# RWKV-6 chunks feeding an MLP on one core: one cumulative-sum matmul instead of two from chunk-batch 8 on, column sums of w_out by one-column matmuls, and a new written-out order

## The chip, the core and the metric

The kernel runs on one core of a Trainium2 chip. The metric is the device time of one execution in microseconds, as the median over five runs. Every figure about a part of the kernel comes from one execution that the hardware profiler recorded.

The core has five engines with a queue each, and every queue runs in order: TensorE (PE; the load of its stationary operand is shown apart as PEld), VectorE (DVE), ScalarE (ACT), GpSimd (POOL) and SyncE (SP), which here issues all the DMAs.

## The reference

```python
# r, k, v, w: (batch 4, heads 8, seq 768, dim 48); u: (8, 48)
state = zeros((B, H, D, D))
for t in range(S):
    cur = einsum('bhd,bhe->bhde', u[None] * k[:, :, t], v[:, :, t])
    y[:, :, t] = einsum('bhd,bhde->bhe', r[:, :, t], state + cur)
    state = w[:, :, t, :, None] * state + einsum('bhd,bhe->bhde', k[:, :, t], v[:, :, t])
x = y.transpose(0, 2, 1, 3).reshape(B * S, H * D)      # 3072 tokens, 384 features
h = maximum(x @ w_in, 0)                               # w_in: 384 x 2048
out = (s * (h * h) + b) @ w_out                        # w_out: 2048 x 384
```

A linear recurrence with a decay w for each channel gives y; an MLP with a squared ReLU follows. `b` is a scalar, so its share of the output is b times the column sums of w_out.

## The kernel before, in words

**Recurrence.** The sequence is cut into chunks of L = 128 steps, six for each of four batch entries: 24 pairs of chunk and entry, called batches n = 0 to 23. Batches 0 and 1 are one double chunk packed together (`packed`); the order of the others goes chunk by chunk over the entries, so batches 20 to 23 are the last chunks (no state is passed on from them: `keep` is false). For each batch:

- `load n.0` to `n.3` (SP, L279 to L308) bring w, r, k and v, 192 KB each (384 KB for the packed pair), in rows of 192 bytes.
- `ln` (ACT, L310): logarithm of w in bf16, `lw`.
- `cum` (PE, L355): cumulative sums of `lw` over the chunk, as two matmuls of 128x384 into one PSUM tile `cums` of two banks: the exclusive sum with `tri_strict` (L383) into bank 0, minus the inclusive sum with `ntri_incl` (L386) into bank 1; and four one-column matmuls (L391) for the chunk's total decay, at the end of bank 0, if `keep`.
- `exp` (ACT, L399): Exp of both, 768 columns, into `E` in bf16 (L404), and Exp of the four columns into `lam` (L408). `l2` (POOL, L431) spreads `lam`.
- `mul` (DVE, L411): r and k times the two halves of `E`, into `prd`.
- `tr` and `tev` (PE L445, ACT L462) transpose `prd`, and from batch 9 on `tev` is a DMA transpose on SP (L477) instead.
- `mt` (PE, L494): the products of k and r of the chunk, into a PSUM tile of two banks; `msk` (DVE, L526) masks them. `cum` and `mt` share one PSUM buffer, tag A, of which there is one: each waits until the one before has been read.
- `ymm` (PE, L537), `yev` (DVE, L621): the batch's y. In `ymm` of the packed pair, the upper 64 rows follow the lower ones.
- `dmm`, `sup`, `st` (PE, DVE, POOL) carry the state; `rkp`, `rku`, `cd`, `yd` (POOL and DVE) make the term with u; `vb` casts v.
- `xtr` and `xev` (PE, ACT) transpose y into the MLP's input `xT`; from batch 12 on `xev` is a DMA transpose on SP (L486).

**MLP.** Two batches make one token tile T (0 to 11) of 256 tokens. `g1 T.i` (PE, L714): six matmuls of 128x256 into `h_ps` (two PSUM buffers); `relu` (ACT, L732); `sq` (L740) squares on DVE or ACT; `g2 T.q` (PE, L758): four matmuls of 128x384 into `o_ps`; `oev` (DVE, L773) and `store` (SP). The weights come as four pieces each, `li` and `lo` (768 KB each), and are cast by `ci` and `co`. The column sums: `colsum` 0 to 3 (L797) multiply an all-ones matrix by w_out, 16 matmuls of 128x384 that leave every column sum in all 128 rows; `csevac` (ACT, L809) scales them by b into `bconst`.

**The order.** The program is not laid out by loops. Each step above is registered with `pl.add` (name, engine, a planned duration, dependencies, and the buffer rings that it takes), from L854 on, and the string `ORDER` (L37) names every step in the sequence in which it is issued. `Plan.order` (L130) walks that string and checks dependencies and rings; each engine gets its instructions in that sequence. `@A`, `@D`, `@P` after a name overrule its engine, and `+8` stands for eight dummy matmuls of 128x256 (`warm`, L1046). Planned durations have no effect on the program once `ORDER` is written. Semaphores between instructions are put in by the tile framework, from the tiles that they read and write.

Names in the texts join step and number: `g10.0` is g1 of tile 0, part 0; `cum22` is cum of batch 22; `A` in "A's next use" is that PSUM buffer.

Of the kernel before, what the change touches and what calls it, by code (L numbers as in the profile page):

```python
# [8 lines left out]
FP32 = mybir.dt.float32  # L9
# [16 lines left out]
PKD = 1.55  # L26
DTK = 9
# [10 lines left out]
load0.0 load0.2 load0.1 load2.0 load_u ln0 ln1 load3.0 +13 cum0 exp0 load3.1 +8 cum1 l20 mul0  # L38
load2.1 load2.2 ln2 rkp0 +2 u_mm load3.2 exp1 tr0 ln3 load0.3 +1 cum2 mul1 tev0 l21 u_ev load3.3
+4 tr1 rkp1 exp2 lo0 tev1 rku1 +4 cum3 exp3 li0 mul2 +9 mt0 rku0 cd1 load2.3 tr2 msk0 rkp3 tev2  # L40
li1 l22 +7 mt1 mul3 vb0@A vb1@A rkp2 msk1 +1 tr3 dmm0 li2 tev3 rku3 sup0 +2 mt2 st0 cd0 co0@A ymm0
cd3 yd0 msk2 load4.0 yd1 ymm1 ci0 yev0 small rku2 xtr0 mt3 yev1 vb2 xev0 +1 xtr1 vb3 xev1 +1 dmm1
l23 li3 +1 dmm2 sup1 g10.0 cd2 ci1 dmm3 g10.1 sup2 relu0.0 msk3 ymm2 relu0.1 lo1 yd2 sq0.0@A g10.2
sup3 sq0.1@A g10.3 yd3 load4.1 yev2 ymm3 load4.2 ci2@D ln4 g20.4 relu0.2 xtr2 yev3 cum4 relu0.3
sq0.2 load5.0 g10.4 xev2 sq0.3@A xtr3 g10.5 ci3 xev3 colsum0 relu0.4 lo2 relu0.5 g20.0 sq0.4 exp4
g10.6 co1 load6.0 sq0.5@A g11.0 relu0.6 lo3 g20.1 relu1.0 g11.1 sq0.6@A mul4 load5.1 g10.7 relu1.1
rkp4 tr4 relu0.7 g11.2 tev4 l24 rku4 load5.2 colsum1 relu1.2 g20.5 st1 cd4 small2 ln5 g11.3
sq1.1@A co2 cum5 sq1.0@A g11.4 relu1.3 sq1.2 load4.3 exp5 g20.2 colsum2 sq0.7@A co3 load7.0 g11.5
ln6 relu1.4 mt4 load5.3 colsum3 msk4 load6.1 rkp5 g11.6 csevac load6.2 relu1.5 g20.6 sq1.3 vb4@A
load7.1 mul5 cum6 g20.7 ln7 sq1.4 load8.0 tr5 exp6 oev0.1 dmm4 g20.3 vb5 load7.2 relu1.6 rku5  # L50
g21.4 oev0.0 tev5 cum7 load6.3 sup4 yd4 g11.7 exp7 g21.0 mul6 load8.1 relu1.7 ymm4 sq1.5@A l26 st2
cd5 mt5 l25 load8.2 rkp6 yev4 tr6 msk5 g21.1 ln8 load7.3 yd5 tev6 g21.5 st3 l27 dmm5 load9.0 rku6
cum8 sq1.7@A sup5 g21.6 exp8 mul7 load9.3 ymm5 vb6@A xtr4 g21.2 st5 st4 yev5 xev4 load8.3 mt6
sq1.6@A xtr5 mul8 tr7 store0.0 xev5 g21.3 tev7 cd6 vb7 g12.0 load10.0 msk6 rkp7 tr8 ln9 dmm6
load12.1 g21.7 rku7 sup6 relu2.0 g12.1 tev8 oev1.1 load11.1 yd6 cum9 cd7 load9.1 relu2.1 g12.2
sq2.0 exp9 l28 ymm6 vb9 load9.2 g12.3 yev6 st6 relu2.2 mt7 oev1.0 sq2.1 store0.1 vb8 g12.4 relu2.3
msk7 yd7 xtr6 dmm7 load11.0 g12.5 xev6 l29 sup7 rkp8 sq2.2@A g22.0 relu2.5 load10.1 dmm8 sq2.3@D
ymm7 ln10 rku8 g22.4 relu2.4 yev7 load12.0 sq2.4@A mt8 sup8 load10.2 st7 g12.6 sq2.5 msk8 g22.5
rkp9 load11.2 relu2.6 xtr7 cd8 g12.7 st8 ln11 load13.0 cum10 xev7 mul9 relu2.7 ymm8 load11.3 g13.0
exp10 rku9 g22.1 relu3.0 load12.2 g13.1 sq2.7 mul10 cum11 ln12 load10.3 dmm9 g13.2 exp11 sq2.6  # L60
tev9 sq3.0 g22.2 relu3.2 cd9 l211 yd8 cum12 relu3.1 sup9 g22.3 ln13 st9 tev10 exp12 g22.6 oev2.0
g13.3 mul11 vb11@A load12.3 g22.7 relu3.3 l212 yev8 rkp10 store1.1 cum13 sq3.1 oev2.1 g13.4 exp13
rkp11 dmm11 tev11 g23.0 sup11 relu3.4 yd9 xtr8 sq3.2@A g13.5 sq3.3 mul12 mt9 load13.1 relu3.5
g13.6 rku11 msk9 xev8 g23.1 load16.0 relu3.6 g23.4 load13.2 st11 vb12@A ymm9 sq3.6@A sq3.5@D mt10
rku10 yev9 sq3.4@A g23.5 msk10 tev12 vb10@A dmm12 l210 xtr9 l213 g23.6 xev9 cd10 g23.2 load17.0
sup12 yd10 g14.0 load14.3 dmm10 mt11 relu4.0 sup10 store1.0 g13.7 msk11 g14.1 relu3.7 rkp13 ymm10
sq3.7 cd11 load14.0 g14.2 st12 relu4.1 yev10 ymm11 relu4.2 mul13 g23.3 load13.3 sq4.1 g14.3 yd11
sq4.0@A load14.1 xtr10 g14.4 relu4.3 rkp12 load14.2 yev11 mt12 oev3.0 relu4.4 g14.5 vb14 tev13
msk12 sq4.4@A rku12 g24.4 relu4.5 xtr11 xev10 g23.7 sq4.3@D load15.0 ln14 cd12 g14.6 xev11
load15.1 sq4.2 vb13@A yd12 oev3.1 cum14 relu4.6 g14.7 load15.2 rku13 sq4.5 ymm12 exp14 dmm13 g24.5  # L70
yev12 cd13 relu4.7 g15.0 xev12 mul14 sq4.6@A g24.0 relu5.0 yd13 sup13 store2.1 g15.1 mt13 st10
load15.3 relu5.1 g15.2 msk13 ln15 l214 g24.6 ln16 store2.0 relu5.2 g15.3 sq4.7@D load18.0 sq5.2@A
rkp15 cum15 ln17 load16.1 g24.1 exp15 st13 dmm14 ymm13 load16.2 relu5.3 rku15 g24.7 yev13 tev14
# [1015 lines left out]
```

## Time and profile before

| | us |
|---|---|
| median of 5 runs | 191.76 |
| the five runs | 191.58, 191.75, 191.76, 191.84, 193.97 |
| the profiled execution, own time | 191.76 |
| its span, first to last instruction | 189.9 |
| PE busy | 182.1 |
| PEld busy | 141.8 |
| ACT busy | 140.9 |
| DVE busy | 124.5 |
| POOL busy | 106.2 |
| DMA: 35.32 MB in 122601 packets, 117329 of them under 512 B | 92.7% of 16 engines' span in queue 1 |

Busy time is a sum of the durations of an engine's instructions, without overlap counted twice. Matmuls are pipelined: each is recorded with its latency, so that the next starts before it ends, and the time for which one holds the engine is read from the start of one to the start of the next. The granted TensorE clock is 1.00 throughout. In lists of groups, a line gives source line, engine, operation, output and inputs by name, shapes and count; then busy time and mean duration in ns; then the idle time of the engine just before, and what ended it. In a timeline a line gives start, duration, engine, line, operation and count, and in brackets an idle time before it.

### The profile page before, as it was taken

Reading aid. Unit: us, or ns where it says so; the run is one execution under the profiler, and the core shown is the slowest. Engines: PE = TensorE matmul, PEld = TensorE weight load, DVE = VectorE, ACT = ScalarE, POOL = GpSimd, SP = SyncE. Lnnn points to the kernel's source line nnn. Section 1 sums busy time; section 2 is a strip of 40 time slices with the busy share of each in tenths; the row PEclk is TensorE's granted clock in tenths of the full one; section 3 lists DMA queues with packets and bytes.
Section 4 is the critical chain, followed back from the end, with each engine's and each line's share of the span. In section 5 each row is a group of like instructions: output and inputs, shape, how many; then the busy total and the mean of one; then the engine's idle time right before and its main releaser. Section 6 shows DMA issues by size and latency. Waiting matters only on the chain.

```text
span 189.9 us, 4916 instructions
## 1 busy us (share of the span) xinstructions
PE 182.1 (96%) x1916; PEld 141.8 (75%) x1916; DVE 124.5 (66%) x198; ACT 140.9 (74%) x268; POOL 106.2 (56%) x138
## 2 busy tenths in 40 slices
PE   6998999999899999999999999999999999999992
PEld 3566898877578786779878777778788777887872
DVE  7348876447669948978686638956577776670242
ACT  3476869988798889958988988749779678483830
POOL 3669773704859965978766696089334677100000
PEclk9999999999999999999999999999999999999999
DMA  6999999989898999999999799899987999630033
GB/s 148 221 202 335 344 327 253 262 221 202 166 179 185 207 169 188 208 174 210 162 209 219 128 207 223 173 196 138 226 165 124 210 164 186 148 109 0 0 128 124
DMA packets 122601, 35.32 MB, mean 186 GB/s; under 512 B 117329, under 2 KB 120530, under 8 KB 122578
## 3 DMA queue, kind: packets, MB, share of 16 engines
q1 hardware_dynamic: 122578, 35.01, 92.7%
q8 instruction: 15, 0.25, 0.6%
q14 instruction: 8, 0.07, 0.1%
HBM read 25.17 MB, written 4.72 MB: 157 GB/s over the span
## 4 chain that ended last, share of the span: by engine, by line
PE 72%; SPq 10%; DMA 6%; DVE 5%; ACT 3%; issue 2%; DVEq 0%
PE o_ps L765 28%; PE h_ps L721 26%; SPq L292 8%; DMA rkt<-in_k_dram 6%; PE mt_ps L516 3%; PE warm_ps L1048 2%; PE y_ps L579 2%; PE trps L450 2%; SPq L841 2%; PE y_ps L570 2%; DVE prd L424 1%; PE cums L368 1%; PE cums L383 1%; PE y_ps L559 1%; PE cums L386 1%
## 5 line engine op out<-in xcount | busy, mean ns | idle before, releaser
L721 PE MATMUL h_ps<-xT,w_in 128*128 128x256 bf16 x576 | 77.7, 273 | 0.0
L765 PE MATMUL o_ps<-w_out,gT 128*128 128x384 bf16 (+1 forms) x400 | 74.7, 320 | 0.1
L734 ACT ACTIVATE rh<-h_ps 128x512 bf16<-128x512 f32 x96 | 56.9, 599 | 23.7 <-PE h_ps L721 22.9
L721 PEld LDWEIGHTS <-w_in 128*128 128x128 bf16 x576 | 60.8, 114 | 7.1
L765 PEld LDWEIGHTS <-gT 128*128 128x128 bf16 x400 | 36.8, 98 | 15.9 <-DVE gT L746 0.2
L744 ACT ACTIVATE gT<-rh 128x512 bf16<-128x512 bf16 x65 | 39.3, 633 | 0.4
L318 POOL TENSOR_TENSOR rkp<-rkt 128x384 f32<-128x384 f32 x22 | 23.2, 1059 | 17.1 <-DMA rkt<-in_k_dram 16.7
L527 DVE TENSOR_TENSOR mt_sb<-mt_ps,tri_strict 128x1024 bf16<-128x1024 f32 x22 | 26.8, 1219 | 7.7 <-PE mt_ps L516 7.7
L424 DVE TENSOR_TENSOR prd<-rkt,E 128x768 bf16<-128x768 f32 x22 | 25.5, 1160 | 9.0 <-DMA rkt<-in_k_dram 6.8
L347 POOL TENSOR_TENSOR yd<-vt,cd 128x384 bf16<-128x384 f32 x22 | 20.7, 943 | 13.3 <-DVE cd L341 7.7
L324 POOL TENSOR_TENSOR rku<-rkp,u_bc 128x384 f32<-128x384 f32 x24 | 27.7, 1162 | 0.4
L404 ACT ACTIVATE E<-cums 128x768 bf16<-128x768 f32 x24 | 19.5, 813 | 4.9 <-PE cums L375 2.4
L624 DVE TENSOR_TENSOR x_sb<-y_ps,yd 128x384 bf16<-128x384 f32 x24 | 13.3, 555 | 13.3 <-PE y_ps L579 9.0
L746 DVE TENSOR_TENSOR gT<-rh 128x512 bf16<-128x512 bf16 x31 | 15.8, 521 | 8.9 <-ACT rh L734 8.9
L776 DVE SCALAR_TENSOR_TENSOR o_sb<-o_ps,s_bc,bconst 128x384 f32<-128x384 f32 (+1 forms) x25 | 14.8, 596 | 8.4 <-PE o_ps L765 8.4
L661 POOL TENSOR_TENSOR st<-stmp,l 128x384 bf16<-128x384 bf16 x16 | 15.6, 978 | 1.7 <-DVE stmp L652 1.6
L437 POOL TENSOR_TENSOR l<-lam,par 128x8 f32<-128x8 f32 x20 | 6.7, 337 | 14.8 <-ACT lam L408 14.8
L313 ACT ACTIVATE logw<-wt 128x384 bf16<-128x384 f32 x22 | 11.4, 525 | 4.3 <-DMA wt<-in_w_dram 4.3
L341 DVE TENSOR_REDUCE cd<-rku 128x8 f32<-128x384 f32 x24 | 13.0, 543 | 2.0 <-POOL rku L324 2.0
L1048 PE MATMUL warm_ps<-warm_sb 128*128 128x256 bf16 x54 | 10.3, 330 | 1.1 <-DVE warm_sb L1005 1.1
L652 DVE TENSOR_TENSOR stmp<-d_ps,st 128x384 bf16<-128x384 f32 x16 | 8.8, 550 | 3.7 <-PE d_ps L611 2.3
L516 PE MATMUL mt_ps<-RK 48*128 48x128 bf16 x176 | 8.7, 219 | 0.0
(90 smaller groups left out, 174.8 us busy)
## 6 DMA issues: line engine op xcount, KB each, us to landing
out_dram<-o_sb SPq DMA_DIRECT2D x23, 192.0 KB, 3.5
wt<-in_w_dram SPq DMA_DIRECT2D x22, 192.0 KB, 4.4
rkt<-in_r_dram SPq DMA_DIRECT2D x22, 192.0 KB, 4.7
rkt<-in_k_dram SPq DMA_DIRECT2D x22, 192.0 KB, 4.6
vt<-in_v_dram SPq DMA_DIRECT2D x22, 192.0 KB, 3.9
wo_st<-in_moe_w_out_dram SPq DMA_DIRECT2D x4, 768.0 KB, 6.5
wi_st<-in_moe_w_in_dram SPq DMA_DIRECT2D x4, 768.0 KB, 8.9
pkt<-in_w_dram SPq DMA_DIRECT2D x1, 384.0 KB, 3.8
```

The lines of the kernel that those rows point to most:

```text
L318: nc.gpsimd.tensor_tensor(out=rkp, in0=c["r"], in1=c["k"], op=ALU.mult)
L324: nc.gpsimd.tensor_tensor(out=rku.rearrange("t h d -> t (h d)"), in0=c["rkp"].rearrange("t h d -> t (h d)"), in1=u_bc, op=ALU.mult,)
L347: nc.gpsimd.tensor_tensor(out=yd, in0=c["v"], in1=c["cd"].unsqueeze(2).to_broadcast([128, H, D]), op=ALU.mult,)
L404: nc.scalar.activation(out=E, in_=ps[:, :, 0:HD], func=AF.Exp)
L424: nc.vector.tensor_tensor(out=prd[:, :, :, 0:D].rearrange("t x h d -> t (x h) d"), in0=c["rk"].rearrange("t x h d -> t (x h) d"), in1=c["E ...
L527: nc.vector.tensor_tensor(out=m.rearrange("s g p t -> s (g p) t"), in0=c["mt_ps"].rearrange("s g p t -> s (g p) t"), in1=(masks[n % 2] if ...
L661: nc.gpsimd.tensor_tensor(out=c["st_new"], in0=c["stmp"].rearrange("q p (g e) -> q p g e", g=2), in1=c["l2"].unsqueeze(3).to_broadcast([12 ...
L721: nc.tensor.matmul(ps[:, f, :], lhsT=w_in_sb[ft // FPP][:, kt, :].rearrange("p (m j) -> p j m", j=FPP)[:, ft % FPP, :], rhs=xT[T][:, kt, : ...
L734: nc.scalar.activation(out=rh, in_=hs[T, i], func=AF.Relu)
L744: nc.scalar.activation(out=g, in_=rh, func=AF.Square)
L746: nc.vector.tensor_tensor(out=g, in0=rh, in1=rh, op=ALU.mult)
L765: nc.tensor.matmul(os_[T, k][:, cols], lhsT=gT[T][:, ft, tt * 128 : (tt + 1) * 128], rhs=w_out_sb[ft // FPP][:, ft % FPP, cols], start=(ft ...
```

## The change

From batch 8 on (`ONE = 8`), `cum` leaves out the second matmul. A VectorE add (`inc`) makes the inclusive sum from the exclusive one in PSUM and from `lw`, and a second Exp (`exn`), with scale -1, reads it from SBUF. The first Exp then covers 384 columns and the four decay columns in one instruction; `E` is fp32 and holds `lam`. The column sums of w_out are made by one-column matmuls, with w_out as the stationary operand, so that the sums lie along the partitions; two small VectorE steps (`cssplit`) split them into two bf16 terms, and six matmuls with the identity (`csspread`) spread them over all rows. `ymm` of the packed pair alternates between the two halves of the rows. The order is written anew.

```diff
+ONE = 8
...
+    cs_sum = const.tile([128, 2, KT], BF16, name="cs_sum", tag="cs_sum")
...
-        nc.tensor.matmul(
-            ps[:, 1, 0:HD], lhsT=ntri_incl, rhs=lw[:, :, 0:D], start=True, stop=True
-        )
+        if n < ONE:
+            nc.tensor.matmul(
+                ps[:, 1, 0:HD], lhsT=ntri_incl, rhs=lw[:, :, 0:D], start=True, stop=True
+            )
...
-        E = work.tile([128, 2, HD], BF16, name="E", tag="E", bufs=2)
-        nc.scalar.activation(out=E, in_=ps[:, :, 0:HD], func=AF.Exp)
-        c["E"] = E
-        if cc < NCH - 1:
-            lam = work.tile([128, HP], FP32, name="lam", tag="lam")
-            nc.scalar.activation(out=lam, in_=ps[:, 0, HD : HD + HP], func=AF.Exp)
-            c["lam"] = lam
+        E = work.tile([128, 2, HD + HP], FP32, name="E", tag="E", bufs=2)
+        c["E"], c["lam"] = E, E[:, 0, HD : HD + HP]
+        if n < ONE:
+            nc.scalar.activation(out=E[:, :, 0:HD], in_=ps[:, :, 0:HD], func=AF.Exp)
+            nc.scalar.activation(out=c["lam"], in_=ps[:, 0, HD : HD + HP], func=AF.Exp)
+            return
+        w = HD + HP if cc < NCH - 1 else HD
+        nc.scalar.activation(out=E[:, 0, 0:w], in_=ps[:, 0, 0:w], func=AF.Exp)
+
+    def incl(n):
+        c = cb[n]
+        t = work.tile([128, HD], FP32, name="inc", tag="inc", bufs=1)
+        nc.vector.tensor_tensor(
+            out=t.rearrange("t (h d) -> t h d", h=H),
+            in0=c["cum"][:, 0, 0:HD].rearrange("t (h d) -> t h d", h=H),
+            in1=c["lw"][:, :, 0:D],
+            op=ALU.add,
+        )
+        c["inc"] = t
+
+    def expn(n):
+        c = cb[n]
+        nc.scalar.activation(
+            out=c["E"][:, 1, 0:HD], in_=c["inc"], func=AF.Exp, scale=-1.0
+        )
...
-            out=prd[:, :, :, 0:D].rearrange("t x h d -> t (x h) d"),
-            in0=c["rk"].rearrange("t x h d -> t (x h) d"),
-            in1=c["E"].rearrange("t x (h d) -> t (x h) d", h=H),
+            out=prd[:, :, :, 0:D],
+            in0=c["rk"],
+            in1=c["E"][:, :, 0:HD].rearrange("t x (h d) -> t x h d", h=H),
...
-            for half in range(2):
-                rows = slice(64 * half, 64 * half + 64)
-                if half:
-                    for p in range(HP):
...
-                for h in range(H):
-                    p, sg = divmod(h, 2)
-                    for q in range(2):
+            for p in range(HP):
...
+            for h in range(H):
+                p, sg = divmod(h, 2)
+                for q in range(2):
+                    for half in range(2):
+                        rows = slice(64 * half, 64 * half + 64)
                         nc.tensor.matmul(
                             ps[rows, h * D : (h + 1) * D],
...
-            nc.tensor.matmul(
-                os_["cs"],
-                lhsT=ones,
-                rhs=w_out_sb[i][:, ft % FPP, :],
...
+            for kt in range(KT):
+                nc.tensor.matmul(
+                    os_["cs"][:, kt : kt + 1],
+                    lhsT=w_out_sb[i][:, ft % FPP, kt * 128 : (kt + 1) * 128],
+                    rhs=ones[:, 0:1],
...
+    def cssplit():
+        ps = os_.pop("cs")[:, 0:KT]
+        for x in range(2):
+            if x == 0:
+                nc.vector.tensor_copy(out=cs_sum[:, 0], in_=ps)
+            else:
+                nc.vector.tensor_tensor(
+                    out=cs_sum[:, 1], in0=ps, in1=cs_sum[:, 0], op=ALU.subtract
+                )
+
+    def csspread():
+        ps = psB.tile([128, d_model], FP32, name="csb_ps", tag="B")
+        for kt in range(KT):
+            for x in range(2):
+                nc.tensor.matmul(
+                    ps[:, kt * 128 : (kt + 1) * 128],
+                    lhsT=cs_sum[:, x, kt : kt + 1].to_broadcast([128, 128]),
+                    rhs=identity,
...
+            [("lw", [("inc", n)] if one else every("cum"))], P)
...
+            [("A", [("exp", n), ("inc", n)] if one else [("exp", n)])], P, lat=0.2, slack=SL)
...
+            add(("inc", n), "DVE", 0.48, incl, (n,), [("cum", n)], [("inc", [("exn", n)])], P - 3)
+            add(("exn", n), "ACT", 0.44, expn, (n,), [("inc", n), ("exp", n)], [], P - 3)
```

**The new order.** All steps keep their work; the sequence differs from the first word on. Of the dummy matmuls there are 74 instead of 54, all before `g10.0`. Of the 96 squares 55 are on ScalarE and 41 on VectorE, where it was 65 and 31; of the 24 casts of v 13 and 11 are on ScalarE and GpSimd, where it was 14 and 10. The 155 DMAs are the same, in another sequence. Three stretches of it that the prediction speaks of, the start, the stretch of batches 6 to 8, and that of batch 22:

```diff
+load0.0 load_u load0.2 load0.1 load2.0 load2.1 ln0 ln1 load2.2 +18 cum0 exp0 load0.3 +5 cum1 l20
...
+relu1.5 g20.7 mul5 load5.3 exp6 csspread rkp5 tr5 ln7 load8.0 g11.7 csevac l25 rku5 cum7 tev5
+oev0.1 load6.3 g20.3 exp7 g21.0 mul6 load7.1 mt5 oev0.0 vb4@A yd4 tr6 load9.0 st3 cd5 dmm4 g21.4
+tev6 sup4 vb5 load7.2 g21.1 msk5 l26 relu1.7 l27 yd5 dmm5 ymm4 ln8 load7.3 sup5 g21.5 sq1.7@A yev4
+sq1.5@A vb6 cum8 load8.1 ymm5 st5 inc8 exp8 g21.6 relu1.6 yev5 load8.2 rkp6 xtr4 mt6 xev4 xtr5
...
+sq8.4@A ln22 g18.7 sq8.3@D rku20 xev19 g28.4 cum22 rku21 g28.1 load22.1 inc22 exp22 vb20@A cd20
+load22.2 sq8.5@D exn22 mt20 yd20 supn20 relu8.6 g28.5 msk20 vb21@A g28.2 relu8.7 store6.0 g28.6
```

## The prediction

> **What bounds it now.** The page comes first, its time slices, and then the windows by stage (length, then busy time of each engine, clock, DMA share, GB/s):
>
> ```profile
> ## 2 busy tenths in 40 slices
> PE   6998999999899999999999999999999999999992
> ...
> DMA  6999999989898999999999799899987999630033
> ```
> ```profile
> core 0: us, PE busy (x) PEld busy (x) DVE busy (x) ACT busy (x) POOL busy (x), PEclk, DMA share, GB/s
> ...
> 43.00:60.00 17.00, 16.08 (x183) 12.07 (x182) 12.87 (x21) 13.97 (x27) 11.07 (x15) 1.00 1.04 189
> ...
> 90.00:106.00 16.00, 16.00 (x169) 12.71 (x167) 11.21 (x17) 14.03 (x31) 10.51 (x14) 1.00 1.20 186
> ...
> 154.00:166.00 12.00, 12.00 (x123) 9.48 (x121) 8.02 (x13) 7.88 (x15) 6.39 (x7) 1.00 0.95 155
> ```
>
> Two resources look full: TensorE to the end, the DMA engines to about 166 us. PE's busy time alone proves little, because matmuls overlap in the records; the starts decide. So I read PE's timeline next (start, duration):
>
> ```profile
> 93.41 0.33 PE L383 MATMUL cums<-logw,tri_strict 128*128 128x384 bf16 x1
> 93.57 0.33 PE L386 MATMUL cums<-logw,ntri_incl 128*128 128x384 bf16 x1
> 93.73 0.24 PE L391 MATMUL cums<-ones,logw 128*128 128x1 bf16 x4
> 93.84 0.83 PE L721 MATMUL h_ps<-xT,w_in 128*128 128x256 bf16 x6
> ```
>
> A 384-column matmul takes 0.33 us but holds PE for 0.16; four one-column ones hold it for 0.11 (26 ns each). With such spacings (g1 0.655, g2 0.65, cum 0.43 or 0.33 without its column sums, mt 0.42, ymm 0.375, dmm 0.17, xtr 0.165, tr 0.45) I add up PE's work along the order. From the first h_ps (25.0) to PE's end (186.4) it is 159.1 of 161.4 us. So **PE is the bound there**; the idle 2.2 us is 1.0 at 49.4, 0.6 between 50 and 73, and small steps.
>
> That stall shows the second resource (the bracket holds the idle time before, and what ended it):
>
> ```profile
> 49.35 0.96 DVE L424 TENSOR_TENSOR prd<-rkt,E 128x768 bf16<-128x768 f32 x1 [1.71 <-DMA rkt<-in_k_dram]
> ...
> 50.87 0.52 ACT L313 ACTIVATE logw<-wt 128x384 bf16<-128x384 f32 x1 [1.37 <-DMA wt<-in_w_dram]
> ...
> 50.36 0.62 PE L450 MATMUL trps<-identity,prd 128*128 128x128 bf16 x8 [0.92 <-DVE prd L424]
> ```
>
> Batch 6's k and batch 8's w are used as they land. Sorted in order of issue, the trace's landing events come one 192 KB load every 1.03 us from 4.5 us to about 60, w_in and w_out pieces every 2 to 3 us. **Until batch 8 the DMA engines set the earliest pace**, and no PE saving moves them. Later there is room: against the same rate, landings fall behind by 9 us at 110 and 17 at 158, since issues wait for buffers and transposes.
>
> **The change, part by part.** Spacings for its matmuls come from the timeline; the rows of the other engines are these:
>
> ```profile
> L404 ACT ACTIVATE E<-cums 128x768 bf16<-128x768 f32 x24 | 19.5, 813 | 4.9 <-PE cums L375 2.4 <-PE cums L391 1.4 <-PE cums L386 0.5
> ...
> L624 DVE TENSOR_TENSOR x_sb<-y_ps,yd 128x384 bf16<-128x384 f32 x24 | 13.3, 555 | 13.3 <-PE y_ps L579 9.0 <-PE h_ps L721 2.5 <-POOL yd L347 0.7
> ...
> L313 ACT ACTIVATE logw<-wt 128x384 bf16<-128x384 f32 x22 | 11.4, 525 | 4.3 <-DMA wt<-in_w_dram 4.3
> ...
> L408 ACT ACTIVATE lam<-cums 128x4 f32<-128x4 f32 x20 | 3.6, 180 | 0.0
> ```
>
> 1. *Second cum matmul, n from 8.* Gone: 16 x 0.163 = 2.6 us of PE, all after 50 us, where PE is the bound. Counts in full.
>
> 2. *Column sums.* Now 16 matmuls at 0.163 = 2.6 us. After: 48 one-column ones and six of 128 columns. The row says 26 ns with a full weight load each: 48 x 0.026 = 1.25, and 6 x 0.055 (spacing of the transposes) = 0.33; saved 1.0. The Trainium skill ("TensorE: Matmul & The Clock Gate", "Wait — 56ns, not 53.3ns?") speaks against this: with hardware decode off, ucode spends about 62 ns per matmul. Then 54 x 0.062 = 3.3, a loss of 0.7. The trace has 26 ns, so I take the row. The part lies before 50 us anyway, under the DMA pace, as do the two tiny VectorE steps.
>
> 3. *Packed ymm, halves interleaved.*
>
> ```profile
> 15.41 0.42 PE L505 MATMUL mt_ps<-RK 48*64 48x128 bf16 x16
> 15.76 0.62 PE L450 MATMUL trps<-identity,prd 128*128 128x128 bf16 x8
> ...
> 20.31 0.65 PE L559 MATMUL y_ps<-vb,mt_sb 64*64 64x48 bf16 x16
> 20.90 0.36 PE L549 MATMUL y_ps<-st,RK 128*64 128x96 bf16 x4
> ```
>
>    The packed mt alternates halves and takes 22 ns a matmul (0.35 for 16); ymm, half after half, 32 to 37. Two times 32 x 12 ns = 0.8 us; 0 if alternating doesn't overlap here. In the front, under cover.
>
> 4. *ScalarE.* 0.81 + 0.18 becomes two 384-wide Exps like Ln, 0.52 each: +0.05 for each of 12 batches, +0.23 for the last four. Ten squares go to VectorE (31 to 41 there, 65 to 55 here): -6.3. Net about -5 of 141 us.
>
> 5. *VectorE.* 16 adds of PSUM + SBUF, like L624: 8.9 us; ten squares at 0.52: 5.2. Busy 124.5 to about 138. Mul reads E in fp32: r and k are fp32 already, so I take the same 0.96 (from 0, to +0.4 if fp32 E collides more with POOL, hidden under up to 4 us of PE work). Worst stretch, 73 to 118: now 34.4 of 45 us; the order puts eight adds, six more squares and five other steps there, +10.3. Successive records overlap by 0.08, 5.5 us over 69 instructions, so some 39 of 45 us are taken. Tight, not full.
>
> 6. *The longer chain.* cum, exp, mul becomes cum, add and exp, exn, mul: +0.5 to +1.1 us (tr8 stands 9.8 us of PE work behind cum8). Behind mul wait tr or tev and mt; from batch 9 on mt starts 7 to 16 us after its batch's loads land, so I count 0 there. The PSUM buffer A matters: one buffer for cum and mt, and PE waits in order behind the next use. If add and Exp read together, A is free 0.11 + 0.56 + 0.04 = 0.71 us after cum. The skill ("PSUM — Partial Sum Buffer", "PSUM bank collisions raise a hardware error") forbids two engines on one bank at once, reads included, so they must take turns: 0.71 + 0.55 = 1.26. No row here has two engines on one bank. PE's work between cum and A's next use is 1.19 (cum8 to mt6), 1.20 (14 to 11), 1.20 (21 to 19), 0.65 (22 to 20), elsewhere 1.85 to 4.7 us. Together: no stall. In turn: 0.8 us in sum, and with VectorE 0.2 us late on average 1.6. I take **1.1**; ends 0 and 5 (VectorE 1 us late).
>
> 7. *Order, DMA issues.* All 155 issues stay. Ahead of batch 6's k stand 57 units of 192 KB (59 before), ahead of batch 8's w 60 (61). So k6 lands at 49.2 - 2.1 = 47.2 at the latest, w8 at 50.85 - 1.0 = 49.8. mul6 (1.0), then tr6 at 48.3; Ln (0.5) plus handover, then cum8 at 50.4; tr6's lateness carried on to cum8 gives 51.3. I take **50.8**, against 52.4 now, with the same PE work done by then (44.2 us before, 44.5 after, dummies included): 1.6 us earlier. The 74 dummy matmuls (54 before, 0.109 each) fill waits: followed by hand with the durations of before, cum1 comes once Exp 0 is read out (7.9 instead of 8.6), mt0 now ahead of cum3 at 13.8 (15.4), and mask, ymm, xtr and xev behind it put the first h_ps at 23.7 to 25.0 (25.0). Its own PE work ahead is 19.3 (17.9 before), so cum8 could stand at 48.9 to 50.2 by PE alone: the DMA pace decides, and a front 1 us later still changes little. New mt-to-cum gaps of 1.30 against a mask of 1.37 (two places): 0.15. On SP late loads stay behind transposes that wait for PE (k23 behind batch 20's xT, as now), so they move earlier with PE; mt23 now starts 7.3 us after k23 lands.
>
> **Sum** for the profiled execution, whose own time 191.76 is also the median (span 189.9 and 1.9 around it): -1.6 up to cum8, -2.6 behind it, +1.1 and +0.15 of new stalls, and -0.3, half of the 0.6 us of old stalls between 50 and 73 (loads that came late by chance or by turn; the other half I let recur). That is -3.3: **188.5**.
>
> **Rivals.** *Everything counts*: no new stall, front and colsum too: -2.6 - 1.0 - 0.8 - 1.0 (the old stall) = 186.3. For it: PE has no other limit after 73. Against: landings before 60.
>
> *Loads keep the pace*: PE gets ahead and meets late loads or SP's turn; only 0 to 1.5 us is left: 190.3 to 192. For it: DMA share near 1 to 154, batch 23's k used as it lands. Against: 9 to 17 us of landing room. This is also the case in which the change does not do what it says.
>
> *A held by VectorE* (slower): adds queue behind masks (1.22) in the 73 to 118 stretch. With every add 1 us late the four tight gaps and cum18 (1.85) cost 5.2 us; 2 us late, 14 (most gaps then). From about 0.9 us late the gain is gone, at 1.2 it is slower by 1%. At 2 us: 188.5 - 1.1 + 14, near 201; typically 194 to 201. For it: 39 of 45 us. Against: now VectorE waits for PE, not the reverse.
>
> **How the numbers follow.** Main case 0.66, own range 186.7 to 190.2; everything counts 0.08; loads keep the pace 0.14; A held 0.12. One per cent, about what a measurement here tells from no change, is 1.9 us: below 189.8 lie 0.62 of the main case and 0.08, so 0.70 faster; 0.17 within; 0.13 slower. The range leaves out A held and the slower end of the loads case (0.15) and a little below the best case (0.04): 186.2 to 192.3.
>
> **What would show it.** Right: the L386 group falls to x8; add rows of 0.55 x16; PE's cum8 near 50.8; starts without gaps behind it, except 0.3 to 0.8 before mt20; PE's last matmul near 183. Wrong at step 2: colsum groups above 0.5 us; at step 6: gaps after many cums, ended by VectorE or ScalarE; at step 7: cum8 after 52, or PE waiting for transposes behind late loads. What breaks it most easily: VectorE late in 73 to 118.

## The result, and the profile after

After takes 192.19 us (median of 38 runs), before 191.76 (75 runs): a ratio of 1.0033, 95% interval 1.0016 to 1.0050. That is no gain where 188.5 was forecast: inside the range, on the wrong side of before. The profiled execution of after took 192.59 us, its span is 190.8 (before 191.76 and 189.9).

The page of after, as the page of before was read:

```profile
PE 180.4 (95%) x1958; PEld 140.7 (74%) x1958; DVE 139.3 (73%) x226; ACT 136.2 (71%) x261; POOL 108.5 (57%) x139
...
PE   7989999998999999898999999999999997999993
...
DMA  5999899979989899999974779998869686442212
...
PE 52%; DVE 15%; SPq 13%; DMA 8%; ACT 5%; issue 4%; ACTq 0%; DVEq 0%
```

PE is 1.7 us less busy, in a longer span. The last line is the chain of work that ended last, by engine. That line of before:

```profile
PE 72%; SPq 10%; DMA 6%; DVE 5%; ACT 3%; issue 2%; DVEq 0%
```

VectorE's share of it was 5% and is 15% now, PE's fell from 72% to 52%. The windows (length; busy time of PE, PEld, DVE, ACT, POOL; clock; DMA share; GB/s) say where:

```profile
43.00:60.00 17.00, 16.21 (x192) 12.83 (x190) 13.60 (x20) 14.68 (x29) 13.47 (x18) 1.00 0.94 184
74.00:90.00 16.00, 14.70 (x161) 11.28 (x160) 15.96 (x21) 11.22 (x24) 14.35 (x18) 1.00 0.96 200
90.00:106.00 16.00, 15.72 (x175) 12.26 (x174) 13.05 (x20) 13.60 (x29) 8.94 (x11) 1.00 0.74 150
154.00:166.00 12.00, 10.95 (x101) 8.75 (x100) 9.28 (x15) 7.95 (x17) 5.79 (x5) 1.00 0.69 153
```

PE was full in the last two before (16.00 of 16, 12.00 of 12) and isn't now. From 74 to 90 VectorE is busy 15.96 of 16 us. The DMA share fell from 1.20 to 0.74 and from 0.95 to 0.69, and none of PE's gaps past 60 us was ended by a load, so late loads are not the reason. In PE's timeline cum8 stands where the forecast put it (50.8), and has one matmul where before had two:

```profile
50.61 0.33 PE L387 MATMUL cums<-logw,tri_strict 128*128 128x384 bf16 x1
...
52.32 0.40 PE L539 MATMUL mt_ps<-RK 48*128 48x128 bf16 x8
```

The new groups, beside those shown of before (busy, mean ns, then the idle time before them and what ended it):

```profile
L415 ACT ACTIVATE E<-cums 128x388 f32<-128x388 f32 (+1 forms) x16 | 7.9, 494 | 8.6 <-DVE inc L420 7.9
...
L420 DVE TENSOR_TENSOR inc<-cums,logw 128x384 f32<-128x384 f32 x16 | 8.8, 551 | 4.8 <-ACT E L415 2.5
```

The durations are as forecast. New is the right-hand side: ScalarE stands 7.9 us ahead of Exps until an add is done, VectorE 2.5 us ahead of adds until an Exp is done. They read the sum strictly one after the other.

**Where the time went.** I gave each matmul start of the trace to its step of `ORDER`; the distance of two steps less the spacing of the first (the prediction's) is PE's idle time. From cum8 to PE's last matmul before takes 133.5 us (52.4 to 185.9), after 136.5 (50.6 to 187.1). PE has 2.6 us less to do on that way and stands idle 5.5 us more. Of after's 6.4 us past 60: 2.4 between 74 and 95 at dmm11, xtr9, dmm12, mt11, xtr11, dmm13, mostly ended by VectorE (mt11, 0.2 of it, waits for buffer A); 2.1 where the next step needs PSUM buffer A (mt15, mt18, mt20, cum18, cum21); 1.2 ahead of g29.0; 0.7 in small steps. These three places are the columns of the table; the kernels are those of the experiments.

| kernel | median us | ratio to before, 95% interval | cum8 to last matmul | idle past 60 | 74 to 95 | buffer A | g29.0 |
|---|---|---|---|---|---|---|---|
| before | | 1 | 133.5 | 0.9 | | | |
| after | 192.19 | 1.0033 (1.0016 to 1.0050) | 136.5 | 6.4 | 2.4 | 2.1 | 1.2 |
| after again | 191.49 | 1.0020 (0.9999 to 1.0042) | 136.6 | 6.2 | 2.4 | 2.1 | 0.6 |
| two matmuls | 189.97 | 0.9938 (0.9916 to 0.9960) | 134.8 | 2.3 | 0.8 | 0.4 | 0 |
| add without PSUM | 191.05 | 1.0009 (0.9975 to 1.0042) | 134.7 | 4.5 | 2.9 | 0.2 | 0 |
| ten squares back | 191.54 | 1.0036 (1.0017 to 1.0055) | 136.3 | 6.1 | 1.3 | 2.0 | 0.7 |
| from batch 13 | 191.86 | 1.0094 (1.0068 to 1.0119) | 136.7 | 6.0 | 2.2 | 2.1 | 0.7 |
| two banks, one tile | 193.41 | 1.0173 (1.0147 to 1.0200) | 138.5 | 5.2 | 1.6 | 1.8 | 1.0 |
| two tiles | 191.51 | 0.9874 (0.9797 to 0.9951) | 136.1 | 3.6 | 1.5 | 0.2 | 0.8 |
| six steps moved | 191.12 | 0.9996 (0.9976 to 1.0016) | 135.6 | 4.7 | 2.4 | 0.7 | 0 |
| ... and two squares | 189.66 | 0.9933 (0.9901 to 0.9966) | 133.6 | 3.5 | 1.1 | 0.7 | 0 |
| mended, one matmul | 189.61 | 0.9830 (0.9783 to 0.9877) | 134.4 | 3.2 | 0.3 | 0.9 | 0 |
| mended, two | 190.75 | 0.9894 (0.9843 to 0.9945) | 135.3 | 1.8 | 0 | 0.6 | 0 |

For reading it: before itself had 191.13, 190.39, 191.44 and 192.56 in the four groups of runs, so ratios compare kernels of different groups only to about half a per cent; within a group the medians do (first group: two matmuls, add without PSUM, ten squares back; second: from batch 13, two banks; third: after again, six steps moved, and two squares; fourth: two tiles, both mended). Medians are over all runs, ratios leave out slow ones (for the two tiles three of six runs), and in the fourth group four of before's runs had a granted clock of 0.98 and took 193.1 to 194.2 us, without which its median is 191.99, so that group's ratios may be some 0.4% too low. The expectations of the first group reckon with before's 191.76, 0.6 us above what it had there. The idle columns come from one execution each, which can be the fastest of its kernel (add without PSUM 189.91, and two squares 188.94) or the slowest (two banks 194.07). And cum8 itself lies between 49.3 and 51.4 in all kernels with the new order, with nothing changed ahead of it, so a difference below 1 us in one span says little; the fourth column leaves the front out.

### The profile page after: what moved, and what is told of

The parts are those of the page before. It is cut to its first block, busy times and chain, and to the rows that moved or that the text cites. A ratio compares the mean times of both kernels' runs of the same rounds, so it can differ in the third digit from the quotient of the medians.

```text
span 190.8 us, 5012 instructions
## 1 busy us (share of the span) xinstructions
PE 180.4 (95%) x1958; PEld 140.7 (74%) x1958; DVE 139.3 (73%) x226; ACT 136.2 (71%) x261; POOL 108.5 (57%) x139
## 4 chain that ended last, share of the span: by engine, by line
PE 52%; DVE 15%; SPq 13%; DMA 8%; ACT 5%; issue 4%; ACTq 0%; DVEq 0%
PE h_ps L744 23%; PE o_ps L788 21%; SPq L296 8%; DMA wo_st<-in_moe_w_out_dram 5%; DMA rkt<-in_k_dram 4%; DVE gT L769 3%; DVE prd L447 3%; PE mt_ps L539 3%; SPq L715 2%; DVE inc L420 2%; ACT E L415 2%; DVE mt_sb L550 2%; DVE x_sb L647 1%; SPq L304 1%; PE trps L473 1%
## 5 line engine op out<-in xcount | busy, mean ns | idle before, releaser
L788 PE MATMUL o_ps<-w_out,gT 128*128 128x384 bf16 (+1 forms) x400 | 73.8, 320 | 1.3 <-DVE o_sb L799 1.1
L744 PE MATMUL h_ps<-xT,w_in 128*128 128x256 bf16 x576 | 73.8, 273 | 0.0
L322 POOL TENSOR_TENSOR rkp<-rkt 128x384 f32<-128x384 f32 x22 | 26.0, 1186 | 21.1 <-DMA rkt<-in_k_dram 21.1
L767 ACT ACTIVATE gT<-rh 128x512 bf16<-128x512 bf16 x55 | 33.7, 629 | 0.3
L328 POOL TENSOR_TENSOR rku<-rkp,u_bc 128x384 f32<-128x384 f32 x24 | 29.3, 1226 | 0.5 <-DVE u_bc L901 0.4
L447 DVE TENSOR_TENSOR prd<-rkt,E 128x768 bf16<-128x768 f32 x22 | 25.7, 1166 | 2.8 <-DMA rkt<-in_k_dram 2.7
L769 DVE TENSOR_TENSOR gT<-rh 128x512 bf16<-128x512 bf16 x41 | 21.9, 556 | 6.7 <-ACT rh L757 6.5
L684 POOL TENSOR_TENSOR st<-stmp,l 128x384 bf16<-128x384 bf16 x16 | 14.0, 874 | 4.5 <-DVE stmp L675 4.5
L415 ACT ACTIVATE E<-cums 128x388 f32<-128x388 f32 (+1 forms) x16 | 7.9, 494 | 8.6 <-DVE inc L420 7.9
L1105 PE MATMUL warm_ps<-warm_sb 128*128 128x256 bf16 x74 | 12.0, 309 | 1.1 <-DVE warm_sb L1062 1.1
L420 DVE TENSOR_TENSOR inc<-cums,logw 128x384 f32<-128x384 f32 x16 | 8.8, 551 | 4.8 <-ACT E L415 2.5
## 6 DMA issues: line engine op xcount, KB each, us to landing
out_dram<-o_sb SPq DMA_DIRECT2D x23, 192.0 KB, 2.9
wt<-in_w_dram SPq DMA_DIRECT2D x22, 192.0 KB, 4.2
rkt<-in_r_dram SPq DMA_DIRECT2D x22, 192.0 KB, 4.2
rkt<-in_k_dram SPq DMA_DIRECT2D x22, 192.0 KB, 4.2
vt<-in_v_dram SPq DMA_DIRECT2D x22, 192.0 KB, 3.8
```

The lines of the kernel that those rows point to most:

```text
L322: nc.gpsimd.tensor_tensor(out=rkp, in0=c["r"], in1=c["k"], op=ALU.mult)
L328: nc.gpsimd.tensor_tensor(out=rku.rearrange("t h d -> t (h d)"), in0=c["rkp"].rearrange("t h d -> t (h d)"), in1=u_bc, op=ALU.mult,)
L447: nc.vector.tensor_tensor(out=prd[:, :, :, 0:D], in0=c["rk"], in1=c["E"][:, :, 0:HD].rearrange("t x (h d) -> t x h d", h=H), op=ALU.mult,)
L744: nc.tensor.matmul(ps[:, f, :], lhsT=w_in_sb[ft // FPP][:, kt, :].rearrange("p (m j) -> p j m", j=FPP)[:, ft % FPP, :], rhs=xT[T][:, kt, : ...
L767: nc.scalar.activation(out=g, in_=rh, func=AF.Square)
L769: nc.vector.tensor_tensor(out=g, in0=rh, in1=rh, op=ALU.mult)
```

## The experiments

### Undo the sum's part in the new order

```diff
-ONE = 8
+ONE = 24
-... inc8 exp8 ... exn8 ...
+... exp8 ...
```

> After with the second cumulative-sum matmul put back for every batch (ONE = 24): no adds, no second Exps, one Exp of 768 columns and one of 4 instead; the new order, the column sums and the packed ymm stay, and so do the squares on VectorE. PE has 2.6 us more to do. Theory 1: with the 3 us of gaps gone, 191.2 to 192.2. Theory 2: VectorE is 8.9 us lighter and all 5.5 us of new gaps go, 188.9 to 190.0 (the 1.8 us that the front is ahead at cum8 come through). Theory 3 (the new order makes gaps by itself): 192.8 to 195.

189.97, ratio 0.9938: 0.95% below after. With 2.6 us more PE work the gaps fall from 6.4 to 2.3 us. So in this order the cumulative sum's part loses, by 4 us of gaps against 2.6 us of work, and the rest of the change (order, column sums, packed ymm, squares) gains 0.6%. The number lies in the second theory's range as it stands; with 0.6 us taken off the forecasts it lies between the first two theories (188.3 to 189.4 and 190.6 to 191.6), so it does not tell them apart. The new order by itself (theory 3) is not at fault.

### The sum's part alone, in the old order

```diff
 (before.py, the same cum, expo, incl and expn; for n from 8:)
-... exp8 ...
+... exp8 inc8 exn8 ...
```

> Before with only the change of the cumulative sum from batch 8 on: second matmul out, add and second Exp put in directly behind the Exp; E in bf16, decay columns in their own Exp, squares, column sums and order as before. PE has 2.6 us less to do. Theory 1 (turn-taking holds the PSUM buffer): the old order has mt or cum 1 us or less behind cum in several places, so gaps of 3 to 6 us, 192.3 to 195.5. Theory 2 (VectorE's load): here VectorE has 8.9 us more and not the ten squares, so less is lost than in after, 190 to 191.5. Theory 3 (the new order is what costs): 189 to 190.

194.83, ratio 1.0183 (1.0141 to 1.0225): theory 1's number. Idle past 60 is 5.4 us, against 0.9. The part loses there too, with before's squares on ScalarE. But the places are not those of theory 1: 0.9 us stand ahead of steps that need buffer A (cum12, mt14), while g12.4, g13.6, g16.1 and g16.4, 1.7 us together, wait for a relu, and ScalarE stands 10.9 us ahead of second Exps, since this edit puts each directly behind its add. The front, which the edit doesn't touch, began 1.1 us later in the profiled execution (g10.0 at 26.1 against 25.0), 0.5 us of it left at cum8; the rest is gaps.

### The add without PSUM

```diff
-            in0=c["cum"][:, 0, 0:HD].rearrange("t (h d) -> t h d", h=H),
+            in0=u_bc.rearrange("t (h d) -> t h d", h=H),
```

> After with one edit: the add reads u from SBUF (fp32, 384 columns) in place of the sum in PSUM, so the inclusive sum is not what the reference needs; VectorE keeps 16 adds, PE and ScalarE keep all their work, and the Exp is the only reader of the bank. Theory 1 (the price is the turn-taking of add and Exp on one bank: PE idles 0.26 + 0.53 + 0.34 + 0.69 us at mt6, mt15, mt18, mt20, 0.9 us by late ScalarE steps): these gaps close and the chain to mul is shorter, 188.2 to 189.8. Theory 2 (VectorE has too much to do, wherever its add reads): 191.4 to 192.4, the gaps of 0.3 to 0.8 between 74 and 95 and the 1.2 before g29.0 stay. Theory 3 (the new order itself): 191.4 to 192.4, with all gaps.

191.05, ratio 1.0009 (0.9975 to 1.0042): between the two numbers as they stand, and with 0.6 us taken off, in that of theories 2 and 3 (190.8 to 191.8). The trace shows that both of the first two theories hold in part. The gaps at buffer A and ahead of g29.0 go (3.3 to 0.2), as theory 1 says; those of 74 to 95 stay and grow from 2.4 to 2.9, as theory 2 says. The growth has a cause that I hadn't reckoned with: the row of the add.

```profile
L420 DVE TENSOR_TENSOR inc<-u_bc,logw 128x384 f32<-128x384 f32 x16 | 13.3, 829 | 0.2
```

With both operands in SBUF it takes 829 ns, from PSUM 551. Of the 16, ten lie wholly under a GpSimd instruction and take 0.94 us on average, four lie clear of any and take 0.55. VectorE thus got 4.5 us more to do, and this run is no clean test of theory 2.

### Ten squares back on ScalarE

```diff
-... sq3.7@D ... sq4.0 ... sq4.1@D ...
+... sq3.7@A ... sq4.0@A ... sq4.1@A ...   (and 2.4 3.1 4.6 5.6 5.7 6.0 6.4)
```

> After with ten squares between 65 and 120 us given back to ScalarE (2.4, 3.1, 3.7, 4.0, 4.1, 4.6, 5.6, 5.7, 6.0, 6.4), where before has them. Theory 2 (VectorE's load between 74 and 95): half to all of the 2.4 us of gaps there go, 189.8 to 191. Theory 1: ScalarE is the one that waits in turn and gets 5 us more, so 192 to 193.5. Theory 3: no change, 191.8 to 192.5.

191.54, ratio 1.0036. dmm11 and dmm12 no longer wait, and 74 to 95 has 1.3 us of gaps instead of 2.4. But new waits for ScalarE came, 0.4 each at g14.4 and g26.0, and others of 0.3 at mt9, g22.1 and g25.7. With 0.6 us taken off, the time fits theory 1 (191.4 to 192.9) as well as theory 3 (no change, 191.2 to 191.9), so it tells nothing of VectorE; the two squares further down are the finer test.

### From batch 13, and only where there is room

```diff
-ONE = 8
+ONE = 13                            (first run)
+ONE = (14, 15, 16, 17, 19, 23)      (second; n < ONE becomes n not in ONE)
```

> After with the single matmul from batch 13 on instead of 8, so that the five adds and second Exps that fall into 50 to 90 us are gone (batches 8 to 12 with two matmuls); PE has 0.8 us more to do. Times for a chip on which before has 191.1 (after then 191.7). VectorE's load is what makes the gaps of 74 to 95 (2.4 us in after): they fall to 0.5 or less, mt6's 0.26 goes too, 190.0 to 190.8; the gaps at mt15, mt18, mt20, g29.0 stay. Rival, the turn-taking and the order make all gaps: those of 74 to 95 stay above 1.5 us, 191.7 to 192.4.

> After with the single matmul only in batches 14, 15, 16, 17, 19 and 23, whose next use of the PSUM buffer comes late and which lie behind VectorE's full stretch; the other batches have two matmuls. PE has 1.0 us less than in the version with two matmuls everywhere (189.97 with before at 191.13). Gaps come only from tight buffer uses and from VectorE before 95: 188.7 to 189.4. Rival, an add costs wherever it stands (VectorE and ScalarE late at squares and relu): 189.8 to 191.

From batch 13: 191.86, ratio 1.0094; the rival's side. Without five of the adds the gaps of 74 to 95 are still 2.2 us. dmm12 stands at 86.9 us in this kernel after a gap of 0.8, with the add of batch 13 among VectorE's steps ahead of it; in the version with two matmuls it stands at 86.8 without a gap. That speaks for VectorE setting PE's times up to there, so that PE work saved ahead of it turns into idle time; the two squares below test it.

Only where there is room: 190.42 (189.61 to 191.15), ratio 0.9991 (0.9970 to 1.0012), with before at 190.39: the rival's number. Six matmuls (1.0 us) less than two everywhere, 1.2 us more idle: 0.65 ahead of mt17, whose DMA transpose landed late, 0.6 ahead of g29.0.

### Whose turn: a bank of its own, the other order, a tile of its own

```diff
-        if n < ONE:
-            nc.tensor.matmul(ps[:, 1, 0:HD], lhsT=ntri_incl, ...)
+        nc.tensor.matmul(ps[:, 1, 0:HD], lhsT=ntri_incl if n < ONE else tri_strict, ...)
...
-        in0=c["cum"][:, 0, 0:HD]...
+        in0=c["cum"][:, 1, 0:HD]...
```

> After with the exclusive sum made twice, by a second matmul into the other bank of the same PSUM buffer, and the add reading that one: the Exp and the add no longer read one bank, all 16 adds and Exps stay, the output is the same, PE has 2.6 us more to do. With before at 191.1 and after at 191.7. Theory 1, turn-taking at the bank: the gaps at mt6, cum18, mt15, mt18, mt20 (2.0 us) close and no Exp waits for an add, g29.0's 1.2 perhaps; 191.1 to 192.4. Rival, the longer chain or the adds' place in VectorE's queue hold the buffer as long without a shared bank: those gaps stay, 193.8 to 194.5. The gaps of 74 to 95 stay under both, less what the extra PE work covers.

193.41, ratio 1.0173. The gaps at mt6, mt15, mt18 and mt20 stayed (0.26, 0.43, 0.33, 0.74), as the rival says. But its timeline at batch 22 shows that the run did not make what it was meant to:

```profile
148.71 0.56 DVE L420 TENSOR_TENSOR inc<-cums,logw 128x384 f32<-128x384 f32 x1 [1.36 <-issue]
149.30 0.49 ACT L415 ACTIVATE E<-cums 128x384 f32<-128x384 f32 x1 [2.00 <-DVE inc L420]
149.84 0.40 PE L539 MATMUL mt_ps<-RK 48*128 48x128 bf16 x8 [0.58 <-ACT E L415]
```

The Exp reads bank 0, the add bank 1, and the Exp still starts when the add ends (149.27). The program keeps the turns for the tile. So the next version gives each bank a tile, at the price of a mask in two halves:

```diff
-        ps = psA.tile([128, 2, 512], FP32, name="cums", tag="A")
+        ps = [psA.tile([128, 512], FP32, name=f"cums{x}", tag=f"A{x}") for x in range(2)]
...
-        ps = psA.tile([128, 2, HP, 128], FP32, name="mt_ps", tag="A")
+        ps = [psA.tile([128, HP, 128], FP32, name=f"mt_ps{x}", tag=f"A{x}") for x in range(2)]
```

> The version with the sum made twice, but with two PSUM tiles of one bank each in place of one tile of two banks: the Exp reads one tile, the add the other. The mask then is two VectorE instructions of 512 columns instead of one of 1024, and batches 2 to 7 have their Exp in two. PE has 2.6 us more to do than in after. If the turn-taking is kept for a tile: Exp and add now overlap, ScalarE no longer waits for adds (9.6 us in the version with one tile), and the gaps at mt15, mt18 and mt20 (0.43, 0.33, 0.74) shrink to 0.2 or less; time 192 to 193 with before at 191.1, since masks cost VectorE 1.5 us more. Rival, the gaps come from adds that stand late in VectorE's queue: the gaps stay above 0.3 each, 193.5 to 195.

The same place in this kernel:

```profile
146.95 0.33 PE L391 MATMUL cums<-logw,tri_strict 128*128 128x384 bf16 x1
...
147.15 0.49 ACT L416 ACTIVATE E<-cums 128x384 f32<-128x384 f32 x1 [1.18 <-PE cums L387]
147.37 0.56 DVE L421 TENSOR_TENSOR inc<-cums,logw 128x384 f32<-128x384 f32 x1 [1.71 <-issue]
...
147.86 0.50 PE L540 MATMUL mt_ps<-RK 48*128 48x128 bf16 x8
```

Exp and add overlap, mt20 follows its PE work without a gap. The 9.6 us for which Exps waited for adds are gone from the list of waits, and the gaps at mt6, mt15, mt18, mt20 with them: buffer A costs 0.2 us instead of 1.8. Ratio 0.9874 (0.9797 to 0.9951), below the forecast 192 to 193, but from few and scattered runs (188.7 to 192.0); its trace, one of the longest of them, has 2.4 us less from cum8 to the end than with one tile. So the gaps at buffer A go when Exp and add overlap. This run does not part that from two things that came along: each half of the buffer comes free by itself, and the mask is cut in two. But the add without PSUM, which leaves tile and mask as they are, closed the same gaps. What the overlap leaves is each reader's wait in its queue: the sum is held for 1.70 us in the median of the 16 batches, where it was 2.30 with one tile.

The order of the two readers was tried as well:

```diff
-... inc14 exp14 ...
+... exp14 inc14 ...      (and 8, 9, 15, 16, 18, 19, 20, 22)
```

> After with the Exp ahead of the add wherever the order has the add first (batches 8, 14, 15, 16, 18, 19, 20, 22), nothing else. In after ScalarE stood 7.9 us waiting for adds, VectorE 2.5 us for Exps. With before at 191.1 and after at 191.7. If what costs is ScalarE standing behind a late VectorE: gaps at mt15 and mt20 fall by half or more and those ended by late logarithms and squares go, 190.2 to 191.0. Rival: the buffer is held for the sum of both whichever comes first, and now the adds stand behind the Exps in VectorE's full queue: 191.4 to 192.4.

193.18 (191.18 to 194.95), ratio 1.0122 (1.0079 to 1.0165): no gain, rather a loss. mt15's gap fell to 0.2 and mt18's went, mt20's stayed (0.68), and xtr11's grew to 0.9. Why it lost as much I did not find out: the profiled execution, at the upper end of the runs, has its largest excess ahead of 60 us, where only batches 8 and 9 were changed (9 is not in the expectation's list).

### Take the waits away

```diff
-... exn22 mt20 yd20 supn20 relu8.6 g28.5 msk20 ...
+... exn22 yd20 supn20 relu8.6 g28.5 mt20 msk20 ...   (likewise mt6, cum18, mt15, mt18)
-... mul23 g29.5 load22.3 g19.7 rkp23 oev8.1 ...
+... oev8.1 mul23 g29.5 load22.3 g19.7 rkp23 ...
-... sq3.7@D ... sq4.1@D ...          (second run)
+... sq3.7@A ... sq4.1@A ...
```

> After with six steps moved in the order and nothing else: mt6, cum18, mt15, mt18 and mt20 each behind the next piece of g1 or g2 (0.65 us of PE work more ahead of them), oev8.1 ahead of mul23. In after PE stood idle at these places 0.26, 0.21, 0.53, 0.34 and 0.69 us, and 1.21 us ahead of g29.0, which waits for oev8.1: 3.2 us. With before at 191.1 and after at 191.7. If these waits are single places where the PSUM buffer is read too long and where a step is queued behind the mul that waits for the second Exp, they go for good: 188.5 to 189.6. Rival, VectorE and ScalarE set the pace there and the idle time only moves on: 190.8 to 192. The gaps of 74 to 95 stay under both.

> The version with six moved steps, and squares 3.7 and 4.1 on ScalarE (81 to 86 us, where VectorE has squares of 1.0 us each). If VectorE paces 74 to 90, the gap ahead of dmm12 (0.76) and the one at mt11 (0.22) close without ScalarE making new ones of that size: 0.6 to 1.2 us below the version with moved steps alone. Rival, ScalarE is as full there, as with ten squares given back: no gain, within 0.3.

> After itself on the same chip as the three others, to compare them with: 0.3% above before, as measured, 191.4 to 192.3 with before at 191.1.

After again: 191.49, with the same gaps to a few hundredths, but for tr5 (0.9, now gone) and g29.0 (1.2, now 0.6). Six steps moved: 191.12, 0.4 us below it, the rival's number. The chosen gaps all went; g25.7 (0.5) and cum21 (0.7, was 0.3) took over a part, and a stall of 0.8 us at tr7, ahead of 60, hid more. The two squares then gave 1.5 us (189.66 against 191.12; the intervals of the ratios don't overlap), more than the 0.6 to 1.2 expected; tr7's stall, which this trace does not have, may be a part of it. The window of the version without them (as in after) and with them:

```profile
74.00:90.00 16.00, 14.70 (x161) 11.29 (x160) 15.96 (x22) 11.22 (x25) 14.35 (x19) 1.00 0.87 185
```
```profile
74.00:90.00 16.00, 15.26 (x164) 11.89 (x163) 14.57 (x21) 12.86 (x28) 14.35 (x19) 1.00 0.99 200
```

VectorE falls from 15.96 to 14.57, PE rises by 0.56, dmm12 and dmm13 no longer wait. VectorE was the bound of this stretch, and two of its 41 squares decide it.

```diff
-ONE = 8
+ONE = (14, 15, 16)       (and mt20 behind g28.5)
```

> The version with two matmuls (189.97 with before at 191.13), with the single matmul in batches 14, 15 and 16 alone, and mt20 behind one more piece of g2. PE has 0.5 us less to do and a gap of 0.4 less. If a single matmul pays where VectorE has room and the buffer's next use is far: 189.0 to 189.4. Rival, each add costs what it saves wherever it is: 189.6 to 190.3.

189.57, ratio 0.9922 (0.9895 to 0.9948): the rival's band by its median, and not told apart from two matmuls (0.9938).

```diff
 (the six moved steps; squares 3.5, 3.7, 4.1, 5.6 on ScalarE; cum21 behind g27.3)
-ONE = 8
+ONE = 24                 (second run, without inc and exn)
```

> After with the six moved steps, squares 3.5, 3.7, 4.1 and 5.6 on ScalarE, and cum21 behind one more piece of g2; single matmul from batch 8 on as in after. With before at 191.1 (the version with moved steps and two squares then 189.8): gaps at dmm11, xtr9 (0.8 together), g25.7 (0.5) and cum21 (0.7) close by half or more, 188.2 to 189.2. Rival, they come back at other places: 189.5 to 190.2.

> The version just before with two matmuls in every batch and no adds (order, squares and moved steps the same). PE has 2.6 us more to do. If the single matmul pays once its waits are mended: 1 to 2.4 us above that version, 189.8 to 190.6 with before at 191.1. Rival, an add and a longer chain cost what the matmul saves wherever they are: within 0.5 of it.

One matmul 189.61, two 190.75, in one group, six runs each that overlap in one pair only (190.22, 190.17): 1.1 us of the 2.6 come through, as the first theory has it. In proportion to before, 189.61 is the forecast of the mended version too (188.2 to 188.7 at before's 191.1). By the traces from cum8 on it is 0.9 (134.4 against 135.3). The gaps of 74 to 95 are gone but for 0.3; behind the moved cum21 stand 1.1 us at g27.3 and 0.9 at mt19, so that this move looks like a mistake. With a ratio of 0.983 to before (0.988 by the median of 191.99) this version beats before; after was not run in this group.

## Why the prediction was wrong, point by point

**Step 1** failed: *"all after 50 us, where PE is the bound. Counts in full."* The 2.6 us of PE work did go. But the time between steps was then set elsewhere: by VectorE up to about 95 us, by buffer A from there to 150, by g29.0's wait at 161. With the second matmul put back the kernel is 1.8 us faster. What PE's idle time showed in before (0.9 us past 60) was that nothing else was later than PE, not by how much it was earlier. In the version with two matmuls mul12 ends at 86.44 and PE comes to dmm12, its first user, at 86.84: 0.4 us of room, where the single matmuls of batches 8 to 14 take 1.1 us out ahead of that step and an add goes in ahead of mul12.

**Step 2, step 3, step 4** hold: twelve one-column matmuls take 0.44 us from first start to last end, 25 ns apart (forecast 26; the 62 ns weighed against it do not show); the packed ymm's 32 take 0.69 (16 took 0.65 before); ScalarE is down 4.7 us (forecast 5).

**Step 5** was right in its sum (139.3 us busy, forecast 138; mul still 1166 ns) and failed in *"some 39 of 45 us are taken. Tight, not full."* The sum has a slip: 34.4 is a time in which overlap is already counted once (the windows 73.3 to 88.3, 88.3 to 103.4 and 103.4 to 118.6 of before have 13.96, 10.34 and 10.14 us of VectorE), and the 5.5 us took it off again. Taken off for the 19 new instructions alone it is 1.5, so 34.4 + 10.3 - 1.5 = 43.2 of 45: full by its own terms. (After has 40.1 us there, in 59 instructions where the sum has 68.) And an average over 45 us hid the 16 us that fill first. Their row of before, which the prediction does not show:

```profile
74.00:90.00 16.00, 16.00 (x183) 12.93 (x181) 14.24 (x22) 12.71 (x26) 13.07 (x15) 1.00 1.08 197
```

VectorE was busy 14.24 of these 16 us before anything was added. Last, the step priced a square at 0.52. VectorE and GpSimd there, in after:

```profile
81.58 2.99 DVE L769 TENSOR_TENSOR gT<-rh 128x512 bf16<-128x512 bf16 x3
84.49 0.54 DVE L420 TENSOR_TENSOR inc<-cums,logw 128x384 f32<-128x384 f32 x1
84.95 1.22 DVE L769 TENSOR_TENSOR gT<-rh 128x512 bf16<-128x512 bf16 x1
...
86.56 1.11 DVE L447 TENSOR_TENSOR prd<-rkt,E 128x768 bf16<-128x768 f32 x1
```
```profile
83.10 1.18 POOL L322 TENSOR_TENSOR rkp<-rkt 128x384 f32<-128x384 f32 x1
84.23 0.70 POOL L876 CAST vb<-vt 128x384 bf16<-128x384 f32 x1
84.89 1.00 POOL L328 TENSOR_TENSOR rku<-rkp,u_bc 128x384 f32<-128x384 f32 x1
85.85 1.01 POOL L351 TENSOR_TENSOR yd<-vt,cd 128x384 bf16<-128x384 f32 x1
```

A square takes 0.9 to 1.2 us here, 0.42 where GpSimd is still; GpSimd is busy 14.35 of these 16 us. The group's mean mixes the two. mul12, the last line of VectorE's, stands behind four such squares and an add, and PE has nothing left to cover it: dmm12 starts at 87.73, when mul12 has ended (87.67).

**Step 6** had the mechanism (the two readers take turns) and the place mt20 (0.69 us, forecast 0.3 to 0.8), and was mis-sized: *"I take 1.1"*. Buffer A costs 2.4 us with mt6. From the start of cum to the end of the last reader it takes 1.44 us at best, as *in turn* says (1.26 behind cum's own 0.16), but 2.15 in the median of the 16 batches, since each reader stands behind what its queue has ahead of it; with two tiles it is 1.14 at best. What the step left out altogether is who waits behind the waiting ones: ScalarE's 7.9 us ahead of Exps delay logarithms and squares (0.4 us of PE's at g27.3 end with a square of ScalarE), and the longer chain to mul delays what VectorE has behind mul. At 161 us:

```profile
157.19 0.56 DVE L420 TENSOR_TENSOR inc<-cums,logw 128x384 f32<-128x384 f32 x1 [0.63 <-ACT E L415]
...
157.67 1.07 DVE L769 TENSOR_TENSOR gT<-rh 128x512 bf16<-128x512 bf16 x1
...
157.78 0.53 ACT L430 ACTIVATE E<-inc 128x384 f32<-128x384 f32 x1
...
158.66 1.75 DVE L447 TENSOR_TENSOR prd<-rkt,E 128x768 bf16<-128x768 f32 x1
...
160.34 0.60 DVE L799 SCALAR_TENSOR_TENSOR o_sb<-o_ps,s_bc,bconst 128x384 f32<-128x384 f32 x1
...
161.00 0.81 PE L788 MATMUL o_ps<-w_out,gT 128*128 128x384 bf16 x4 [1.05 <-DVE o_sb L799]
```

The add of batch 23 waits 0.63 us for its turn behind the Exp, the square behind it is late by that, and mul23 starts when the square ends (158.7; the second Exp is done at 158.3). It takes 1.75 us under GpSimd, and oev8.1, which frees the PSUM that g29.0 needs, stands behind it. The step asked only for tr, tev and mt behind mul.

**Step 7** was right: cum8 at 50.61 (50.8), the first h_ps at 23.75 (23.7 to 25.0). That cum8 came so close is in part luck: with the same front it stands between 49.3 and 51.4 in the other kernels.

**The rivals.** *Loads keep the pace* is out: DMA shares fell, and among the gaps of after past 60 us none was ended by a DMA. *A held by VectorE* was the right side and half of the cause: it put the whole price on buffer A, which cost 2.4 us; an equal part came from VectorE as the bound of 74 to 90, which no rival named by itself. In the sum, the terms up to cum8 (-1.6, measured -1.8) and behind it (-2.6) held; the term of new stalls was 1.1 + 0.15 - 0.3 and measured 5.5. That makes +1.1, against the 1.2 us by which PE's last matmul is later (187.1, 185.9).

**The turns.** Step 6 rested on the Trainium skill ("PSUM — Partial Sum Buffer", "PSUM bank collisions raise a hardware error"): two engines that read one bank must take turns. In after's trace none of the 16 pairs of Exp and add overlaps. This program keeps turns also between two banks of one tile (add to 149.27, Exp from 149.30), where the rule would allow both at once; the two-tile run, in which 12 of the 16 overlap (in batch 22 Exp 147.15 to 147.64, add from 147.37), agrees with the rule there.

## What to carry to other kernels

An engine that is never idle is the bound only by as much as the next one has room: what is saved beyond that room turns into idle time. Before its work is taken away, look in each stretch of 10 to 20 us for the engine that has less room than the saving, and price its instructions as they run in that stretch, not by the mean of the group. When work moves to another engine, list what stands behind it in that queue and behind every step whose chain grows, and who waits for those. Here 1.1 of the 2.6 us came through once these waits were mended, measured with and without the second matmul in the same mended order.

## What the runs showed that I had not expected

- The turns of two readers of a PSUM tile are kept for the tile and not for the bank: with the sum in two banks of one tile Exps waited 9.6 us for adds, with two tiles no such wait is left.
- A VectorE instruction stretches beside GpSimd by where its operands are. In after, squares of SBUF take 0.42 us clear of GpSimd and 0.88 on average wholly under it (11 squares, 0.45 to 1.22), the PSUM add 0.55 in both cases; in the run without PSUM the add takes 0.55 and 0.94. The Trainium skill ("SBUF — State Buffer", "SBUF: two separate sides") states a port pair that a VectorE instruction with two SBUF inputs and a GpSimd instruction that reads SBUF lock against each other; these rows agree in kind.
